# Eight layer norms move from the third block of a Fourier layer into the first stage of its fourth block

## The chip, the cores and the metric

The kernel runs on one core of a Trainium2 chip. The metric is device time in microseconds: the median over executions. Before the change it is 1607.54 us, the median of 3 executions from 1606.18 to 1608.23.

## The reference

The program applies four layers to one sequence of S = 2048 rows and D = 512 columns, in f32: two pairs of a Fourier layer (FNet) and a gated feed-forward layer (GEGLU, F = 1792). Each layer normalises its input rows first and adds its result to the input.

```python
def fnet(x, Sre, Sim, Hre, Him):        # y = Re(DFT_seq(DFT_hid(x)))
    a, b = x @ Hre.T, x @ Him.T
    return Sre @ a - Sim @ b
def geglu(x, wg, wu, wd):
    return (gelu(x @ wg) * (x @ wu)) @ wd
x = x + fnet(layernorm(x), ...)         # layer 0
x = x + geglu(layernorm(x), ...)        # layer 1
x = x + fnet(layernorm(x), ...)         # layer 2
x = x + geglu(layernorm(x), ...)        # layer 3
```

`layernorm` takes mean and variance over the 512 columns of a row and has no weights; eps is 1e-5.

## The kernel before

**Products.** Every f32 operand x is split into two numbers, hi (a copy rounded to a narrower type, by ScalarE, line 168; line 194 is the form with the sign turned) and lo = x - hi (by VectorE, line 170; with the sign turned, line 196). A product is three matmuls into the same bank: hi by hi (line 225), hi by lo (226), lo by hi (227), each of a 128x128 weight by 128x512. So a matmul of line 225 needs ScalarE's half alone, and those of 226 and 227 need VectorE's as well. On top of that the kernel multiplies 2x2 blocks of matrices with seven block products in place of eight, for which sums and differences of blocks (VectorE, line 201 plus of SBUF tiles, line 205 the same plus where one operand is a PSUM bank, line 208 minus) are formed on the way. ScalarE copies finished banks out in line 212.

**Layer 2 in blocks.** The function `mix` runs a Fourier layer. Its output rows come in four blocks b = 0 to 3 of 512 rows; the change is about the third (b = 2) and the fourth (b = 3) of layer 2. A block has two stages:

- S2, 24 steps of six matmuls (function `six`): three chains of eight steps (T2, T1, T3), skewed against each other, each with two banks of its own. The rows of the sequence DFT that it multiplies (`ws` in the trace) come by DMA through SP's queue (line 348), and are summed (line 201 and 208), then split. When the first chain ends, ScalarE copies its banks (line 212) and the banks of the second are added to the copies (line 205).
- S4, 16 steps: two chains (B22, T4) into the banks that S2's second and third chain left.

Between the blocks stand products with the hidden DFT (weights `wq`), for two blocks at a time, named P1 to P7. Block 3 has four of P7 early and, after S4, its last products: two each of P4, P7, P4. The operands of P4 and P7 come from the banks that S4 leaves. The remaining twelve (P6, P5, P3) run beside the next layer.

**The next layer's first half.** Layer 3 takes its rows in two halves of 1024. To begin, it needs the first half normalised and transposed (z^T), and that work is done beside layer 2's last blocks. The function `block_steps` makes the pieces, for row tiles i = 0 to 7 of 128 rows:

- `ahead`, a load of row tiles (line 253, 256 KB each): tiles 4 to 7 through POOL's DMA queue, tiles 0 to 3 (called L in the table of the change) through SP's;
- `stats(i)` (A in the table): VectorE takes the statistics of a tile (line 643) and gathers them (645), adds eps (649); POOL raises the result to the power -1/2 (650); VectorE makes the shift (654);
- `norm(i)` (B): ScalarE scales and shifts the tile (line 687), VectorE transposes it in pieces of 32 (line 780) into one of two tiles named `wide`; after the fourth transpose of a tile, POOL issues the write of it, 1 MB, to DRAM (line 783);
- `fetch(c)`, c = 0 to 3: 8 DMAs on POOL (line 794, 64 KB each, four from each of the two writes) that bring a column block of z^T back.

Behind them VectorE forms differences and sums of the fetched tiles, and both engines split them, for layer 3's first products.

**Where they stand.** Two lists spread this work. `chores` is walked by blocks 2 and 3 at 16 places of a block: two early products, eight steps of S4, six late products. `queue` gives one entry per step of matmuls (function `step`). Before, block 2's chores were: the row loads, nothing, then eleven entries of statistics and norms (`NORM_STEPS`); the queue of block 3's S2 held eight empty entries, and then fetches and empty entries by turns. The wrapper `paced` keeps such an entry behind the newest split on ScalarE and VectorE.

**What sets the order.** These lists give the order in the program text. The order on each engine is then set at compile time by a scheduler that goes by a model of the time line, within the data's dependences and the order constraints (`issue_after`, `behind`, `paced`). Each engine works through its own row in order, so whatever waits at its head holds all behind it.

Two other loads touch the place: `xwide` and `wide`, 1 MB each (line 974, four DMAs on SP), bring the layer's old rows back, to which the products of a pair of blocks are added.

Of the kernel before, what the change touches and what calls it, by code (L numbers as in the profile page):

```python
# [21 lines left out]
NT = TB // P  # L22
# [26 lines left out]
PAIRED = {2: ((0, 1), (2, 3))}  # L49
BESIDE = 2  # L50
FURTHER = 4
NORM_STEPS = (
    (("A", 4),), (("A", 5),), (("B", 4), ("A", 6)), (("B", 5), ("A", 7), ("L", 0)), (("B", 6), ("L", 1)),
    (("B", 7), ("A", 0), ("L", 2)), (("A", 1), ("L", 3)), (("B", 0), ("A", 2)), (("B", 1), ("A", 3)), (("B", 2),), (("B", 3),),
)
FIRST_SUMS = 9, 10
LATER = 3
LET = 5
# [6 lines left out]
def fnet_geglu(ctx: ExitStack, tc: tile.TileContext, x_in, ws, wh, wgu, wdn, wdc, whc, out):  # L65
# [32 lines left out]
    nc = tc.nc  # L98
# [73 lines left out]
    def paced(run):  # L172

        def paced_run():
            with tc.issue_after(newest["ACT"].ins), tc.issue_after(newest["DVE"].ins):
                run()
        return paced_run
# [431 lines left out]
    queue, slow, steps_done, pace, down_making = [], [], [0], [PACE], []  # L609
# [264 lines left out]
    def mix(layer):  # L874
        hid, sums, chores, hid_left = {}, {}, [], [0]

        def chores_at(b):
            if b == NB - 3:
                norms, others = block_steps(layer + 1, 0)
                at = 0 if b in paired else NT  # L880
                if not at:
                    ahead = begin[layer + 1, 0, "ahead"]
                    stats = begin[layer + 1, 0, "stats"]
                    both = {("A", i): paced(stats(i)) for i in range(2 * NT)}
                    both.update({("B", i): paced(norms[i]) for i in range(2 * NT)})
                    both.update({("L", i): lambda i=i: ahead(i, 1, nc.sync) for i in range(NT)})

                    def several(*names):
                        return lambda: [both[name]() for name in names]

                    norms = [lambda: ahead(NT, NT, nc.gpsimd), lambda: None]
                    norms += [several(*names) for names in NORM_STEPS]
                later.update(norms=norms[at:], fetches=others[:ND], others=others[ND:])
                return norms[:at]
            if b == NB - 2:
                weights = [weight_steps(n) for n in range(2)] if layer == 0 else []
                norms = later.pop("norms")
                later["others"] += weights[1][1] if weights else []
                return [run for load, _ in weights for run in (load,)] + norms + (weights[0][1] if weights else [])
            return later.pop("others") if b == NB - 1 else []  # L900
# [31 lines left out]
        paired = {b for p in PAIRED.get(layer, ()) for b in p}  # L932
# [24 lines left out]
        def pair_sums():  # L957
            c = sums_due.pop(0)
            u, v = xu.pop(c), xv.pop(c)
            minus(u, cs["P5", c], u)  # L960
            with behind("DVE"):
                nc.vector.scalar_tensor_tensor(v, v, -1.0, u, op0=ALU.mult, op1=ALU.subtract)
            cs["P6", c], cs["P3", c] = u, v
# [60 lines left out]
        def pair_rest(i):  # L1024
            if sums_due:
                pair_sums()
            if i in FIRST_SUMS:
                first_sum(FIRST_SUMS.index(i))
            pair_product(*PAIR_REST[i])
# [106 lines left out]
        sides, us, later = {}, {}, {}  # L1136

        def s2(b):
# [11 lines left out]
            one, three = [ps8.get() for _ in range(2)], [ps8.get() for _ in range(2)]  # L1150
            sides[b] = one, three
            if last:
                queue.extend([None] * (8 if paired else 14) + [run for fetch in later.pop("fetches") for run in (None, fetch)])
            for j, (i, k) in enumerate(skewed(3)):
                if rest_beside(layer, b) and j % BESIDE == 0:
                    pair_rest(j // BESIDE)
# [717 lines left out]
```

## Time and profile before

| | |
|---|---|
| median of 3 executions | 1607.54 us (1606.18 to 1608.23) |
| the profiled execution: its own time, and the span of its instructions | 1609.84 us, 1608.1 us |
| mean granted clock of TensorE | 0.995 of full speed |
| TensorE (PE) busy | 1591.6 us, 99% of the span, 6960 matmuls |
| VectorE (DVE) busy | 1189.1 us, 74% |
| ScalarE (ACT) busy | 881.6 us, 55% |
| GpSimd (POOL) busy | 316.5 us, 20% |
| moved by DMA | 432.79 MB, 269 GB/s over the span |

The profile is one execution. A row that begins with a time is one instruction or a run of equal ones (x6): its start, how long it was busy, the engine, the line of the kernel, and what it reads and writes (out<-in). Square brackets hold the idle time of the engine just before it and what ended that. A row that begins with a line number is a group: how often, its busy time with the mean of one in ns, and the idle time ahead of it with what ended most of it. Tiles carry the names of the program: `s` is any of the 98 work tiles of 128x512, `p` a PSUM bank, `wide`, `rstd`, `shift`, `st` and `mv` are those of the norms. The page gives the span also in 40 slices of 40.2 us, with the busy share in tenths.

### The profile page before, as it was taken

How to read it: one execution, taken by the hardware profiler on the slowest of the kernel's cores; microseconds unless marked ns; L12 is line 12 of the kernel's file. 1: busy time of each engine (PE TensorE's matmuls, PEld its weight loads, DVE VectorE, ACT ScalarE, POOL GpSimd, SP SyncE). 2: the span in 40 equal slices, each digit the busy share in tenths (PEclk: the TensorE clock that was granted, in tenths of full speed). 3: DMA queues.
4: the chain of work that ended last, by engine and by line, in shares of the span. 5: the costliest groups of instructions: out<-in, count | busy, mean ns of one | idle time of the engine just before them, and what ended most of it. 6: DMA issues, size and time to landing. Idle time of an engine off the chain costs nothing.

```text
span 1608.1 us, 22774 instructions
## 1 busy us (share of the span) xinstructions
PE 1591.6 (99%) x6960; PEld 1309.6 (81%) x6960; DVE 1189.1 (74%) x2082; ACT 881.6 (55%) x1687; POOL 316.5 (20%) x533
## 2 busy tenths in 40 slices
PE   9999999999999999999999999998999999999999
PEld 7888888888888888888888888886788888888887
DVE  7997878878699784676868876898795456843573
ACT  8955555654767644656557543545453565333460
POOL 4122322341456101330040000013301000000000
PEclk9999999999999999999999999998999999999999
DMA  9888989976998899997795858787978958996445
GB/s 359 292 328 315 327 307 362 332 263 197 340 322 318 273 322 309 336 345 244 269 304 186 268 169 203 236 271 240 260 268 286 282 170 247 308 277 198 131 144 157
DMA packets 245018, 432.79 MB, mean 269 GB/s; under 512 B 29024, under 2 KB 72288, under 8 KB 243872
## 3 DMA queue, kind: packets, MB, share of 16 engines
q1 hardware_dynamic: 212208, 328.82, 64.1%
q0 software_dynamic: 30000, 100.43, 17.3%
q10 hardware_dynamic: 2688, 2.10, 0.5%
q8 instruction: 55, 0.90, 0.2%
q14 instruction: 67, 0.55, 0.1%
HBM read 333.97 MB, written 97.26 MB: 268 GB/s over the span
## 4 chain that ended last, share of the span: by engine, by line
PE 94%; DVE 2%; DMA 2%; issue 1%; ACT 1%; POOL 0%; SPq 0%; DVEq 0%; POOLq 0%; ACTq 0%
PE p L226 31%; PE p L227 31%; PE p L225 31%; DVE s L170 1%; DMA s<-wq 1%; PE p L1088 1%; DVE s L201 1%; DMA s<-ws 0%; DMA s<-x 0%; PE p L1780 0%; POOL rstd L664 0%; DVE s L205 0%; DVE s L208 0%; DVE wide L780 0%; DVE st L643 0%
## 5 line engine op out<-in xcount | busy, mean ns | idle before, releaser
L226 PE MATMUL p<-s,s 128*128 128x512 f32 x2304 | 896.2, 390 | 4.2 <-DVE s L170 3.5
L227 PE MATMUL p<-s,s 128*128 128x512 f32 x2304 | 890.2, 390 | 0.0
L225 PE MATMUL p<-s,s 128*128 128x512 f32 x2304 | 854.6, 391 | 6.9 <-ACT s L168 4.0
L168 ACT ACTIVATE s<-s 128x512 fp32r<-128x512 f32 (+1 forms) x852 | 480.8, 608 | 299.3 <-DVE s L201 62.2
L170 DVE TENSOR_TENSOR s<-s,s 128x512 fp32r<-128x512 f32 (+1 forms) x852 | 535.9, 661 | 112.1 <-ACT s L168 95.1
L225 PEld LDWEIGHTS p<-s,s 128*128 128x128 f32 x2304 | 433.4, 188 | 100.3 <-ACT s L168 5.7
L226 PEld LDWEIGHTS p<-s,s 128*128 128x128 f32 x2304 | 433.6, 188 | 96.5 <-DVE s L170 5.2
L227 PEld LDWEIGHTS p<-s,s 128*128 128x128 f32 x2304 | 433.6, 188 | 90.5 <-DMA s<-wb 0.3
L205 DVE TENSOR_TENSOR s<-s,p 128x512 f32<-128x512 f32 x211 | 142.3, 682 | 172.1 <-PE p L227 136.3
L201 DVE TENSOR_TENSOR s<-s,s 128x512 f32<-128x512 f32 (+1 forms) x399 | 234.3, 607 | 4.6 <-DMA s<-ws 2.1
L212 ACT ACTIVATE s<-p 128x512 f32<-128x512 f32 x234 | 135.7, 593 | 121.4 <-PE p L227 115.9
L1351 ACT ACTIVATE s<-s 128x512 f32<-128x512 f32 x84 | 52.6, 628 | 42.6 <-DVE s L205 41.7
L334 POOL DMA_DIRECT2D wb<-s x84 | 46.1, 550 | 87.4 <-ACT s L168 68.2
L1351 ACT ACTIVATE s<-p 128x512 f32<-128x512 f32 x28 | 16.7, 597 | 83.3 <-PE p L227 83.3
L687 ACT ACTIVATE s<-s,shift,rstd 128x512 f32<-128x512 f32 x61 | 48.6, 809 | 18.7 <-DVE shift L654 12.3
L1367 DVE TENSOR_TENSOR s<-s,p 128x512 f32<-128x512 f32 x56 | 38.2, 683 | 21.3 <-PE p L227 21.3
L208 DVE TENSOR_TENSOR s<-s,s 128x512 f32<-128x512 f32 (+1 forms) x61 | 36.3, 601 | 22.1 <-DMA s<-ws 17.5
L977 POOL DMA_DIRECT2D x<-wide x8 | 5.2, 658 | 240.3 <-DVE wide L208 240.3
L170 DVE TENSOR_TENSOR s<-xwide,s 128x512 fp32r<-128x512 f32 (+1 forms) x56 | 37.3, 674 | 17.9 <-ACT s L168 12.8
L168 ACT ACTIVATE s<-xwide 128x512 fp32r<-128x512 f32 (+1 forms) x56 | 34.3, 617 | 29.4 <-DVE xwide L205 10.1
L219 ACT ACTIVATE p<-p 128x512 f32<-128x512 f32 x56 | 32.6, 584 | 26.6 <-PE p L227 26.5
L1367 DVE TENSOR_TENSOR s<-s,s 128x512 f32<-128x512 f32 x56 | 38.5, 688 | 1.2
(96 smaller groups left out, 654.0 us busy)
## 6 DMA issues: line engine op xcount, KB each, us to landing
s<-ws SPq DMA_DIRECT2D x368, 256.0 KB, 5.3
s<-wb SPq DMA_DIRECT2D x294, 256.0 KB, 5.2
s<-wc SPq DMA_DIRECT2D x182, 256.0 KB, 4.5
wb<-s POOLq DMA_DIRECT2D x98, 256.0 KB, 4.8
s<-wq SPq DMA_DIRECT2D x56, 256.0 KB, 4.4
s<-x SPq DMA_DIRECT2D x52, 256.0 KB, 5.4
s<-wh SPq DMA_DIRECT2D x52, 256.0 KB, 5.4
wc<-s POOLq DMA_DIRECT2D x49, 256.0 KB, 5.3
```

Source lines behind the costliest of these rows:

```text
L168: newest["ACT"] = nc.scalar.activation(hi, src, AF.Copy)
L170: newest["DVE"] = nc.vector.tensor_tensor(lo, src, f32(hi), op=ALU.subtract)
L201: nc.vector.tensor_tensor(out, a, b, op=ALU.subtract)
L205: bank_read["DVE"] = nc.vector.tensor_tensor(out, a, b, op=ALU.add)
L212: bank_read["ACT"] = nc.scalar.activation(v, src, AF.Copy)
L225: nc.tensor.matmul(ps, ah, bh, start=start, stop=False, skip_group_check=True)
L226: nc.tensor.matmul(ps, ah, bl, start=False, stop=False, skip_group_check=True)
L227: newest["PE"] = nc.tensor.matmul(ps, al, bh, start=False, stop=stop, skip_group_check=True)
L334: nc.gpsimd.dma_start(a, f32(t))
L687: nc.scalar.activation(z, x, AF.Identity, bias=shift, scale=rstd)
L1351: nc.scalar.activation(t, g, AF.Gelu_apprx_tanh)
L1367: nc.vector.tensor_tensor(t, t, v, op=ALU.mult)
```

## The change

The row loads and the statistics of tiles 4 to 7 move to the end of block 2's list (the first eight of its 16 places become empty, then the loads, three empty places, the four statistics). All eight norms, the other four statistics and the loads of tiles 0 to 3 go into a new list, `NORM_LATE`, of twelve entries, which stands at the head of the queue of block 3's S2. The fetches start behind entry 15 of that queue in place of 8.

```diff
-NORM_STEPS = (
-    (("A", 4),), (("A", 5),), (("B", 4), ("A", 6)), (("B", 5), ("A", 7), ("L", 0)), (("B", 6), ("L", 1)),
-    (("B", 7), ("A", 0), ("L", 2)), (("A", 1), ("L", 3)), (("B", 0), ("A", 2)), (("B", 1), ("A", 3)), (("B", 2),), (("B", 3),),
+NORM_STEPS = ((("A", 4),), (("A", 5),), (("A", 6),), (("A", 7),))
+NORM_LATE = (
+    (("B", 4), ("L", 0)), (("B", 5), ("L", 1)), (("B", 6), ("L", 2)), (("B", 7), ("L", 3)),
+    (("A", 0),), (("A", 1),), (("A", 2),), (("A", 3),), (("B", 0),), (("B", 1),), (("B", 2),), (("B", 3),),
 )
+NORM_FROM = 8
+FETCH_AT = 15
@@ chores_at
-                    norms = [lambda: ahead(NT, NT, nc.gpsimd), lambda: None]
+                    norms = [lambda: None] * NORM_FROM + [lambda: ahead(NT, NT, nc.gpsimd)] + [lambda: None] * 3
                     norms += [several(*names) for names in NORM_STEPS]
+                    later["norms late"] = [several(*names) for names in NORM_LATE]
@@ s2
             if last:
-                queue.extend([None] * (8 if paired else 14) + [run for fetch in later.pop("fetches") for run in (None, fetch)])
+                late = later.pop("norms late", [])
+                queue.extend(late + [None] * (FETCH_AT - len(late) if paired else 14) + [run for fetch in later.pop("fetches") for run in (None, fetch)])
```

In the changed kernel the lines above stand three further on (168 becomes 171, 170 becomes 173, 196 becomes 199, 201 becomes 204, 208 becomes 211, 225 to 227 become 228 to 230, 643 becomes 646, 650 becomes 653, 783 becomes 786, 794 becomes 797).

The scheduler answers with another order on every engine. Three places show it. A row gives line, operation, out<-in with the numbers of the tiles, and the shape.

**First place: VectorE at the head of S2 of block 3.** Before (line 643 is a statistic, 196 a lo split for the last of the block before, 201 and 208 sums of S2's rows):

```order
L208 TENSOR_TENSOR s_12355<-s_12353,s_12355 128x512
L208 TENSOR_TENSOR s_12395<-s_12393,s_12395 128x512
L208 TENSOR_TENSOR s_12451<-s_12449,s_12451 128x512
L643 BN_STATS st<-s_12239 128x6
L196 SCALAR_TENSOR_TENSOR s_12350<-s_11947,s_12349 128x512
L643 BN_STATS st<-s_12262 128x6
L643 BN_STATS st<-s_12305 128x6
L196 SCALAR_TENSOR_TENSOR s_12360<-s_11949,s_12359 128x512
L643 BN_STATS st<-s_12322 128x6
L201 TENSOR_TENSOR s_12353<-s_12357,s_12353 128x512
L201 TENSOR_TENSOR s_12393<-s_12397,s_12393 128x512
L201 TENSOR_TENSOR s_12449<-s_12453,s_12449 128x512
```

Now (211, 204, 199 and 646 are those lines, 173 a lo split):

```order
L199 SCALAR_TENSOR_TENSOR s_12271<-s_11949,s_12270 128x512
L204 TENSOR_TENSOR s_12264<-s_12268,s_12264 128x512
L211 TENSOR_TENSOR s_12361<-s_12359,s_12361 128x512
L173 TENSOR_TENSOR s_12366<-s_12280,s_12365 128x512
L204 TENSOR_TENSOR s_12292<-s_12296,s_12292 128x512
L211 TENSOR_TENSOR s_12436<-s_12434,s_12436 128x512
L204 TENSOR_TENSOR s_12268<-s_12266,s_12268 128x512
L204 TENSOR_TENSOR s_12359<-s_12363,s_12359 128x512
L173 TENSOR_TENSOR s_12316<-s_12268,s_12315 128x512
L646 BN_STATS st<-s_12240 128x6
L646 BN_STATS st<-s_12242 128x6
L646 BN_STATS st<-s_12244 128x6
```

Some rows that only repeat line 204 are left out of the second piece. Before, four statistics stood ahead of the first sums of line 201; now sums and two lo splits stand ahead of the first statistic.

**Second place: POOL's row, from the first powers to the last fetch.** Before (650 the powers, 783 the writes of z^T, 794 the fetches, `t_0_1` and `t_0_0` the two halves written):

```order
L650 TENSOR_TENSOR rstd<-rstd,power 128x1 x4
L783 DMA t_0_1_11184<-wide 128x2048
L650 TENSOR_TENSOR rstd<-rstd,power 128x1 x4
L794 DMA s_12622<-t_0_1_11184 32x4x128 x4
L783 DMA t_0_0_11183<-wide 128x2048
L794 DMA s_12687<-t_0_1_11184 32x4x128 x4
```

Now:

```order
L653 TENSOR_TENSOR rstd<-rstd,power 128x1 x4
L786 DMA t_0_1_11184<-wide 128x2048
L653 TENSOR_TENSOR rstd<-rstd,power 128x1
L797 DMA s_12708<-t_0_1_11184 32x4x128 x4
L797 DMA s_12819<-t_0_1_11184 32x4x128 x4
L653 TENSOR_TENSOR rstd<-rstd,power 128x1 x3
L797 DMA s_12780<-t_0_1_11184 32x4x128 x4
L797 DMA s_12742<-t_0_1_11184 32x4x128 x4
L786 DMA t_0_0_11183<-wide 128x2048
L797 DMA s_12703<-t_0_0_11183 32x4x128 x4
```

Before, the second four powers stood ahead of all fetches. Now one of them does, and the other three stand behind eight fetches, which read what the first write writes.

**Third place: TensorE at the last products of block 3** (`p_13138` and `p_13139` are the banks of P4, `p_12839` and `p_12840` those of P7, `p_13242` is the first bank of layer 3). Before, the piece that ends with the two matmuls on `s_13143`, the lo split of an operand of P4 that is made from the banks of S4's chain B22:

```order
L227 MATMUL p_12839<-s_13074,s_12998 128x512
L226 MATMUL p_12840<-s_13075,s_12998 128x512
L227 MATMUL p_12840<-s_13074,s_12998 128x512
L225 MATMUL p_13242<-s_13160,s_13114 128x512
L226 MATMUL p_13242<-s_13161,s_13114 128x512
L227 MATMUL p_13242<-s_13160,s_13115 128x512
L225 MATMUL p_13242<-s_13178,s_13114 128x512
L226 MATMUL p_13138<-s_13143,s_13010 128x512
L227 MATMUL p_13138<-s_13142,s_13010 128x512
```

Now:

```order
L229 MATMUL p_13139<-s_13033,s_12966 128x512
L230 MATMUL p_13139<-s_13032,s_12966 128x512
L228 MATMUL p_13138<-s_13142,s_13010 128x512
L228 MATMUL p_13139<-s_13142,s_13010 128x512
L228 MATMUL p_13242<-s_12853,s_13110 128x512
L229 MATMUL p_13242<-s_12854,s_13110 128x512
L229 MATMUL p_13138<-s_13143,s_13010 128x512
L230 MATMUL p_13138<-s_13142,s_13010 128x512
```

Before, all of P7's last products and 22 matmuls of layer 3 stood ahead of the first use of `s_13143`; now two of layer 3 do, and P7's stand behind. Counted from the last matmul into the first bank of S4's chain B22, 64 matmuls stood ahead of it before, and 32 now.

## The prediction

> **What bounds the kernel now.** I read the page first, then the list of what TensorE waited for, then the time line of the place where it waited. Of the page, the busy line and two of the 40 slices' rows:
>
> ```profile
> PE 1591.6 (99%) x6960; PEld 1309.6 (81%) x6960; DVE 1189.1 (74%) x2082; ACT 881.6 (55%) x1687; POOL 316.5 (20%) x533
> PE   9999999999999999999999999998999999999999
> PEclk9999999999999999999999999998999999999999
> ```
>
> TensorE is the bound, and one slice in 40 (1085 to 1126 us) falls short, in busy time and in granted clock. The waits of TensorE (total, times, longest) and ten-microsecond stretches (first PE busy and its matmuls, then PEld, DVE, ACT, POOL, the clock, DMA) say by how much:
>
> ```profile
> PE p L225 <- ACT s L168: 4.0, 2, 3.3
> PE p L226 <- DVE s L170: 3.5, 2, 2.8
> 1110.00:1120.00 10.00, 6.52 (x14) 4.14 (x14) 8.81 (x23) 6.36 (x12) 8.55 (x8) 0.50 0.09 19
> 1130.00:1140.00 10.00, 10.00 (x45) 8.26 (x44) 7.99 (x13) 4.81 (x8) 6.38 (x12) 1.00 1.06 270
> ```
>
> Fourteen matmuls instead of 45. The time line of TensorE there, at the head of the fourth block's stage S2 (start, duration, idle before and who ended it):
>
> ```profile
> 1094.80 0.39 PE L227 MATMUL p<-s,s 128*128 128x512 f32 x1
> ...
> 1099.56 0.39 PE L227 MATMUL p<-s,s 128*128 128x512 f32 x1
> 1099.79 1.52 PE L225 MATMUL p<-s,s 128*128 128x512 f32 x6
> ...
> 1106.36 0.39 PE L227 MATMUL p<-s,s 128*128 128x512 f32 x1
> 1110.06 1.22 PE L225 MATMUL p<-s,s 128*128 128x512 f32 x2 [3.31 <-ACT s L168]
> 1114.04 0.79 PE L226 MATMUL p<-s,s 128*128 128x512 f32 x1 [2.75 <-DVE s L170]
> ...
> 1122.36 0.80 PE L226 MATMUL p<-s,s 128*128 128x512 f32 x1 [0.75 <-DVE s L170]
> ...
> 1126.36 0.61 PE L227 MATMUL p<-s,s 128*128 128x512 f32 x1
> 1126.79 0.42 PE L225 MATMUL p<-s,s 128*128 128x512 f32 x1
> ...
> 1164.67 0.70 PE L225 MATMUL p<-s,s 128*128 128x512 f32 x2 [1.83 <-DMA s<-wq]
> ```
>
> From 1094.80 to 1099.56 there are 21 steps: 0.2267 us a matmul. After the gap of 3.31 us they come every 0.43 us, at half the clock, until 1126.4. What the other engines did:
>
> ```profile
> 1098.39 1.88 DVE L170 TENSOR_TENSOR s<-s,s 128x512 fp32r<-128x512 f32 x3
> 1103.19 1.28 DVE L643 BATCH_NORM_STATS2 st<-s 128x6 f32<-128x512 f32 x2
> 1107.38 0.37 DVE L645 BATCH_NORM_AGGREGATE mv<-st 128x2 f32<-128x6 f32 x4
> 1107.67 0.66 DVE L201 TENSOR_TENSOR s<-s,s 128x512 f32<-128x512 f32 x1
> 1113.30 1.89 DVE L170 TENSOR_TENSOR s<-s,s 128x512 fp32r<-128x512 f32 x3
> 1121.62 4.29 DVE L170 TENSOR_TENSOR s<-s,s 128x512 fp32r<-128x512 f32 x7
> 1131.24 0.69 DVE L208 TENSOR_TENSOR s<-s,s 128x512 f32<-128x512 f32 x1 [5.33 <-DMA s<-ws]
> 1172.67 1.28 DVE L205 TENSOR_TENSOR s<-s,p 128x512 f32<-128x512 f32 x2 [2.04 <-PE p L227]
> ```
>
> VectorE had no pause from 1098.39 to the sum (1107.67) that the hi split needs, and the lo split came at 1113.30: four statistics (L643) lay between. Seven operations in 4.29 us, the last 0.66 long: 0.605 us each back to back; a small one takes 0.09. That is the bound here: VectorE's queue.
>
> What this stall cost: the six L225 in a row at 1099.79 are found once in the order. From there to the last product of S4's first half, which the pair at 1172.67 reads, the order has 250 matmuls: 56.7 us at 0.2267. They took 72.8. So **16.1 us** are lost in this stretch, 1.83 of them by the wait for wq.
>
> **The change, part by part.** It removes no arithmetic. All eight norms leave the third block's S4 and last products and enter the 24 steps of the fourth block's S2; the thirty-two fetches of z^T come seven steps later. Per norm VectorE does a statistic and a transpose of 0.6 us back to back and three small operations, in all 1.5 us; groups of lines from 1080 to 1180 us:
>
> ```profile
> L780 DVE STREAM_TRANSPOSE wide<-s 128x512 f32<-128x512 f32 x8 | 5.4, 698 | 0.5 <-ACT s L687 0.5
> L643 DVE BATCH_NORM_STATS2 st<-s 128x6 f32<-128x512 f32 x8 | 5.4, 687 | 1.1 <-DMA s<-x 1.1
> ```
>
> Four norms (6 us) go from before the stall to behind it. In exchange the sums of S2 stand ahead of the statistics (first place of the order), and TensorE has 42 instead of 30 matmuls before the first that needs such a sum, so the gap of 3.31 us goes.
>
> *Term 1, S2 itself.* From the last reading of S4's banks to the lo split that the last pair of S2's first chain needs, VectorE's queue now holds 60 large and 21 small operations: 60 x 0.605 + 21 x 0.09 = 38.2 us. It starts at 1098.4 as before, or 2.3 us earlier, since ten matmuls have moved behind S4's end; I take 1097.2. Idle time adds: five shifts that wait for POOL's power, by
>
> ```profile
> 1115.64 0.16 DVE L654 SCALAR_TENSOR_TENSOR shift<-mv,rstd 128x1 f32<-128x1 f32 x1 [0.46 <-POOL rstd L650]
> L650 POOL TENSOR_TENSOR rstd<-rstd,power x4: 548/556/565, 1086.5 to 1089.2; 128x1 f32<-128x1 f32 x4
> L650 POOL TENSOR_TENSOR rstd<-rstd,power x4: 542/626/4659, 1111.0 to 1116.8; 128x1 f32<-128x1 f32 x4
> ```
>
> 5 x 0.46 = 2.3, and a wait for S2's rows behind the 1 MB load of xwide, between 0 and the 5.33 above; I take 2. So 1097.2 + 38.2 + 4.3 = 1139.7, where TensorE, unhindered, would come at 1099.8 + 152 x 0.2267 = 1134.3: **5.4 lost** (bounds: early start, no idle 0; late start, all idle 9.9). The first power took 4.66 us while VectorE ran without a break, the others 0.55 to 0.63.
>
> *Term 2, the chain's end.* S2's first chain ends, ScalarE copies it (line 212), and VectorE adds the second chain's bank to it (line 205). The next matmul writes into that second bank. Before, 29 others stood between (6.6 us); now it comes at once.
>
> ```profile
> L212 ACT ACTIVATE s<-p 128x512 f32<-128x512 f32 x234 | 135.7, 593 | 121.4 <-PE p L227 115.9
> L168 ACT ACTIVATE s<-s 128x512 fp32r<-128x512 f32 (+1 forms) x852 | 480.8, 608 | 299.3 <-DVE s L201 62.2
> ```
>
> A copy, 0.59, and a sum, 0.64, take 1.4 with the hand-overs; two more operations of VectorE stand ahead of the second lo split, 1.2 less one matmul: **2.4** (1.4 to 3.2).
>
> *Term 3, POOL's queue.* The last three powers are now behind eight fetches (second place of the order):
>
> ```profile
> 1115.84 2.93 ACT L687 ACTIVATE s<-s,shift,rstd 128x512 f32<-128x512 f32 x4 [3.00 <-DVE shift L654]
> 1128.76 3.25 POOL L794 DMA_DIRECT2D s<-t  x6 [0.55 <-issue]
> t<-wide POOLq DMA_DIRECT2D x2, 1024.0 KB, 8.8
> s<-t POOLq DMA_DIRECT2D x32, 64.0 KB, 6.3
> ```
>
> The fourth transpose stands behind 48 large and 12 small operations: 1097.2 + 30.1 + four shifts and part of the wait, 3.1, is 1130.4. The write of z^T lands 0.6 + 8.8 later, eight fetches issue in 8 x 0.55, three powers take 1.9, three norms on ScalarE 3 x 0.73 and a split 0.6: 1149. TensorE comes at 1139.7 + 0.9 + 2.4 + 12 x 0.2267 = 1145.7. Behind the waiting shifts stand all of VectorE's splits. **3.3** (0, if the write lands early, to 6).
>
> *Term 4, the last products.* A product of P4 needs a lo split (L196 before, L199 now) of a sum that starts from those finished S4 banks. VectorE's queue holds 19 large operations from the reading of the first of these banks to that split, 11.6 us with the hand-over; before, 18. But before 64 matmuls (14.5 us) stood between on TensorE, and it did not wait; now 32 (7.25 us, third place of the order): 4.4. Two more lo splits behind it cost 1.7 and 1.4 in the same way (17.0 against 15.3, 19.4 against 18.0 us). **7.5** (6.5 to 9.5: the second write of z^T starts near 1151 and lands at 1160, its first fetch 2.2 + 6.3 later at 1168.5; VectorE wants it at 1168, so it may wait up to 2).
>
> *Term 5, the clock.* A gap of 1.83 changed no clock, one of 3.31 did. Term 4's 4.4 us will; half rate there is mostly hidden, as VectorE still sets the pace: **0.8** (0 to 5).
>
> The other late fetches I cost at nothing: the first use of one on VectorE stands 23 large operations behind the chain's end, 1140.6 + 1.4 + 14.1 = 1156, and the third tile, the one it needs, lands at 1146.2 + 2.2 + 6.3 = 1154.7. Without that cover, 1 us late costs 1 us. On SP's queue six loads of wq now stand ahead of the 1 MB load of wide instead of behind it, so I let the 1.83 go; the x rows stand singly among S2's loads, which term 1's wait covers.
>
> Sum: 5.4 + 2.4 + 3.3 + 7.5 + 0.8 = 19.4 lost in place of 16.1 and 0.2 later: +3.1 us. The profiled execution took 1609.84 (span 1608.1), 2.3 over the median of 1607.54; the sum moves all three alike: 1607.5 + 3 = **1610.5 us**.
>
> **The rivals.** *The clock falls twice* (slower). Where the wait in term 1 is one gap of 3.3 us or more, the 28 matmuls that stand behind it run at 0.43. In the trace half rate lasted until 4.0 us of unbroken work were done (1122.36 to 1126.4): 9 matmuls at 0.2 us more are 1.7, and 0.9 more than term 5 has at the end. With xwide's 5.33 in full, 3.3 + 1.7 + 0.9 = 5.9 more: 1616. For it: the clock's fall at 3.31. Against: term 1's waits may come in small pieces. The Trainium skill (TensorE: Matmul & The Clock Gate, Part 1, What's actually happening) puts the point at an idle window of about 3.4 us, which the trace's 3.31 and 1.83 agree with; an estimate from it, half a window lost behind term 4's gap, makes term 5 1.7 and the forecast 1611.4.
>
> *VectorE keeps ahead* (faster). It starts at 1096, loads are there in time, and the powers slip into gaps: term 1 0.9, term 2 2.4, term 3 0.5, term 4 6.5, together 10.3, 6 us less than 16.3: 1601.5. It decides where terms 1 and 3 together stay below 5.4. For it: no x rows in the load queue before S2. Against: 38.2 us of queue over 34.5 us of matmuls. The Trainium skill (GPSIMD Engine Reference, 1. Specifications) says that POOL shares its SBUF interfaces with VectorE and contends with its two-input operations; the 4659 ns agree, and by that rule the powers find no gap, the 2.3 us stay, and this case is 1603.8.
>
> *The stall only moves* (no change): VectorE's large operations from the same start to the split in term 4 are 115 before and 114 now, so if its idle time stays as it was, the end stays: 1607.5.
>
> **How the numbers follow.** The forecast 0.50, with its own range 1607 to 1614; the clock 0.21; VectorE ahead 0.20; only moved 0.09. A range of 1603 to 1616.5 leaves out about a tenth on each side: half of the faster case, half of the clock's. What a measurement here can tell from no change is 0.2%, 3.2 us. Faster by more: the faster case and a little of the forecast's lower end, 0.21. Within: all of the last and 0.28 of the forecast, whose centre lies at +3: 0.37. Slower: the clock's and 0.21 of the forecast, 0.42.
>
> **What would show it.** No wait of 3.3 us for L168 near 1107 (the gain is real); waits at half of S2 and at the chain's end; a wait for the shifts behind the fetches near 1146; a wait of about 4.4 us for the lo split of P4 (now line 199) after 1170, with the clock below 1 behind it. It is wrong if S2 of the fourth block loses under 6 us, or if that last wait is missing: then the change is faster. If VectorE waits for z^T, the fetches decide, not the norms.

## The result and the profile after

The changed kernel takes **1623.79 us** (median of 4 executions, 1620.34 to 1625.14) against 1607.88 for the kernel before on the same chip (4 executions): a ratio of 1.009, 95% interval 1.0068 to 1.0111. It is slower by 15.9 us. The forecast was 1610.5 with a range of 1603.0 to 1616.5, so the direction was right and the size was not: the time lies 7.3 us above the range.

The profiled execution of the changed kernel took 1625.14 us, its span is 1623.4. Its page, the three lines that answer to those shown of before:

```profile
PE 1593.4 (98%) x6960; PEld 1310.8 (81%) x6960; DVE 1190.0 (73%) x2082; ACT 881.4 (54%) x1687; POOL 312.8 (19%) x533
PE   9999999999999999999999999997969999999999
PEclk9999999999999999999999999999989999999999
```

The work of every engine is the same to 4 us. Two slices fall short in place of one, and the deeper one is later: the slice of 1177 to 1218 us, behind S4, where the kernel before had no gap over 0.2 us. The waits of TensorE (total, times, longest):

```profile
PE p L228 <- DMA s<-wb: 12.1, 1, 12.1
PE p L229 <- DVE s L173: 9.1, 4, 6.5
PE p L228 <- DVE s L208: 1.5, 1, 1.5
```

The old wait for line 168's hi split (3.3) is gone, as the prediction said. In its place stand 9.1 us for lo splits, and a wait of 12.1 us that no part of the prediction names: `wb`, a weight of layer 3. The time line of TensorE at these places (start, duration, idle before it and who ended it):

```profile
1111.17 0.50 PE L229 MATMUL p<-s,s 128*128 128x512 f32 x1 [1.58 <-DVE s L173]
...
1134.33 0.80 PE L229 MATMUL p<-s,s 128*128 128x512 f32 x1 [6.50 <-DVE s L173]
...
1148.66 0.47 PE L228 MATMUL p<-s,s 128*128 128x512 f32 x1 [1.50 <-DVE s L208]
...
1192.46 0.76 PE L228 MATMUL p<-s,s 128*128 128x512 f32 x1 [12.05 <-DMA s<-wb]
```

**Where the time went.** From the starts of all matmuls in the two traces one can add up by how much each stands more than 0.2267 us behind the one before it. From 1095 to 1205 us this gives 17.3 us for the kernel before and 33.1 for the changed one, and the difference is that of the spans (15.3) to half a microsecond. The rows leave out steps of under 0.1 us:

| place | before | after |
|---|---|---|
| S2 of block 3, first half and its lo splits, with half clock | 14.3 | 12.0 |
| S2, the chain's end and the late shifts | 0 | 4.8 |
| wait for wq behind the load of wide | 2.0 | 0 |
| end of S4 and first products of layer 3 | 0.6 | 15.9 |

Up to 1175 us both kernels stand level: the matmul that started at 1175 before starts 0.3 us later after. So all the loss is in the last row: 12.05 us of waiting for one weight, and some 3 us at half clock behind it.

**Why that weight was late.** SP's queue, first of the kernel before, then of the changed one:

```profile
1160.80 0.32 SPq L1341 DMA_DIRECT2D s<-wb  x1
...
1166.73 5.52 SPq L1341 DMA_DIRECT2D s<-wb  x11
```

```profile
1163.91 2.32 SPq L978 DMA_DIRECT2D wide<-x  x4
1167.83 1.56 SPq L351 DMA_DIRECT2D s<-wq  x1
1169.49 0.54 SPq L1346 DMA_DIRECT2D s<-wb  x1
1170.12 1.01 SPq L351 DMA_DIRECT2D s<-wq  x1
1171.18 12.68 SPq L1346 DMA_DIRECT2D s<-wb  x9
1184.20 2.40 SPq L351 DMA_DIRECT2D s<-wq  x4
1186.98 1.00 SPq L1346 DMA_DIRECT2D s<-wb  x2
```

The profile's rows don't tell which tile each load fills; the order on SP does (place in the row, line, tile and source; the first number in a name is the work tile, the second numbers the uses):

```
before  913 L1341 DMA s81_13110<-wb0_185 128x512
        917 L1341 DMA s4_13114<-wb0_185 128x512
after   915 L1346 DMA s16_13114<-wb0_185 128x512
        917 L1346 DMA s46_13122<-wb0_185 128x512
        ...
        930 L1346 DMA s7_13110<-wb0_185 128x512
        931 L1346 DMA s9_13111<-wb0_185 128x512
```

`13110` and `13111` are hi and lo of the first weight pair that layer 3 multiplies with. Before, its hi half led the weights, issued at 1160.8. After, ten other weights stand ahead of it; it goes out with its lo half in the pair issued from 1186.98, and TensorE starts again 5.5 us later.

The tiles tell why the scheduler put it there. The list of free tiles hands out the one that was given back first in the program's text, and in both kernels the first weight pair gets tiles into which fetches bring z^T: 81 and 68 before, 7 and 9 after (`s7_12708` and `s9_12780` on POOL's row). The load has to wait until VectorE has read its tile for the last time, and that reading came later. For the hi half's tile, in the order and in the trace:

```
before  L201 s97_12992<-s68_12687,s81_12622
after   L204 s23_12932<-s7_12708,s50_12703
```

```profile
1159.12 0.68 DVE L201 TENSOR_TENSOR s<-s,s 128x512 f32<-128x512 f32 x1
```

```profile
1174.06 0.69 DVE L204 TENSOR_TENSOR s<-s,s 128x512 f32<-128x512 f32 x1 [0.42 <-DMA s<-t]
```

After, the last reading is a sum with a fetch of the second write of z^T, which the late norms moved from 1121 to 1156, and it stands behind the first sum of S4's banks. Tile 9 is read for the last time until 1177.2. Even so both tiles were free some ten microseconds before the pair was issued: what held the load was its place behind ten others in the queue.

The kernel before had no room here either. Its lo half stood thirteenth of the weights, landed at 1179.7, and TensorE's weight load waited 0.3 us for it:

```profile
1179.78 0.19 PEld L227 LDWEIGHTS p<-s,s 128*128 128x128 f32 x1 [0.31 <-DMA s<-wb]
```

### The profile page after: what moved, and what is told of

It is laid out like the page before. It is cut to its first block, busy times and chain, and to the rows that moved or that the text cites. A ratio compares the mean times of both kernels' runs of the same rounds, so it can differ in the third digit from the quotient of the medians.

```text
span 1623.4 us, 22765 instructions
## 1 busy us (share of the span) xinstructions
PE 1593.4 (98%) x6960; PEld 1310.8 (81%) x6960; DVE 1190.0 (73%) x2082; ACT 881.4 (54%) x1687; POOL 312.8 (19%) x533
## 3 DMA queue, kind: packets, MB, share of 16 engines
q0 software_dynamic: 30000, 100.43, 17.3%
## 4 chain that ended last, share of the span: by engine, by line
PE 92%; DMA 4%; DVE 2%; ACT 1%; issue 1%; POOL 0%; SPq 0%; DVEq 0%; ACTq 0%; POOLq 0%
PE p L229 31%; PE p L230 30%; PE p L228 30%; DMA s<-ws 2%; DMA s<-wb 1%; DVE s L173 1%; DMA s<-wq 1%; DVE s L204 1%; PE p L1092 1%; DMA s<-x 0%; ACT s L171 0%; POOL rstd L667 0%; DVE s L211 0%; DVE wide L783 0%; ACT s L690 0%
## 5 line engine op out<-in xcount | busy, mean ns | idle before, releaser
L228 PE MATMUL p<-s,s 128*128 128x512 f32 x2304 | 854.1, 391 | 15.4 <-DMA s<-wb 12.1
```

Of the source, the lines that this page charges most:

```text
L228: nc.tensor.matmul(ps, ah, bh, start=start, stop=False, skip_group_check=True)
```

## The experiments

Each time is a median, each ratio goes against runs of the kernel before on the same chip. The kernel before had medians of 1607.9 to 1609.4 beside them, so ratios compare better than times. Single executions of several kernels spread by up to 0.6%, and a profile is one of them. "Lost" is the sum over matmul starts, as in the table above.

### Other tiles for the first weights

```diff
                 if layer:
+                    ints = [i for i, n in enumerate(sb.free) if isinstance(n, int)][:14]
+                    turn = [sb.free[i] for i in ints]
+                    for i, n in zip(ints, turn[2:] + turn[:2]):
+                        sb.free[i] = n
                     weight_load(0)
```

> The changed kernel, with the free list of work tiles turned by two places just before the fourteen first weight loads of layer 3, so that the first weight pair no longer takes the two tiles that z^T leaves last. SP's row keeps its form, but its first weight load is now the tile that TensorE uses first (in the changed kernel that tile is the eleventh of them). Theory A (tile reuse and order): the wait of 12.1 us for wb at 1180 goes, since the load at this place was issued at 1169.5 and landed some 7 us later. TensorE then meets the lo split of P4, which VectorE ends at 1184.9 in the changed kernel's trace: a wait of about 4 us near 1181, 6 to 8 us lost with its echoes and the clock. Time 1614 us (1611 to 1617), 10 under the changed kernel. Theory B (the loads as a whole are late, since the 1 MB load of wide and sixteen fetches share the DMA engines with them): another weight is late in its place, TensorE waits 8 to 12 us for wb there, and the time stays at 1620 to 1624.

Measured: 1615.65 us, ratio 1.0045 (1.0032 to 1.0058), 8 us under the changed kernel (its profiled execution, 1620.03, is the slowest of five, and 2 us late ahead of S2 already). TensorE's gaps behind S4:

```profile
1182.04 0.47 PE L228 MATMUL p<-s,s 128*128 128x512 f32 x1 [1.42 <-DVE s L173]
1187.47 0.80 PE L230 MATMUL p<-s,s 128*128 128x512 f32 x1 [4.73 <-DMA s<-wb]
```

The hi half came in time; the wait of 12 us became 4.7 for the lo half, which stood fifth of the weights on SP's row. Theory A has the time, but B is not out: a weight was late in its place. (The load at the head of the weights took 11.2 us to land in the changed kernel, not the 7 that the expectation gives it.) Apart from these loads the edit moved twelve matmuls and two operations of ScalarE in the engines' orders, all beside the first weights. The next run gives both halves tiles that are free early, and changes nothing else (against the run above):

```diff
-                    for i, n in zip(ints, turn[2:] + turn[:2]):
-                        sb.free[i] = n
+                    for i, n in zip(ints, (2, 6, 7, 8, 3, 4, 5, 9, 10, 11, 12, 13, 0, 1)):
+                        sb.free[i] = turn[n]
```

> The changed kernel with another permutation of the fourteen work tiles that the first weights of layer 3 take: both halves of the first weight pair now get tiles that are free early, so that they are the first and the second of the weights on SP's row. In the run that turned the list by two, the hi half came first and TensorE still waited 4.7 us for the lo half, which stood fifth. Theory A (which tile the first pair gets, and so its place on SP's row): no wait for wb is left, TensorE goes on to the lo split of P4 and waits there for VectorE alone, 2 to 4 us with half the clock behind it for one or two steps of 3.4 us: 1612 to 1615 us, 1 to 4 below the run that turned the list. Theory B (the loads as a whole are late behind the 1 MB load of wide): the second half waits all the same, 3 to 5 us, 1615 to 1617 us.

Measured: 1615.55 us, ratio 1.0037 (1.0025 to 1.0049); applied to the 1607.9 beside the changed kernel that is 1613.8, in A's range, while the time as measured lies in B's. The step from the run above is not clear of noise, since the two intervals overlap; that from the changed kernel is. The same place in its trace:

```profile
1178.13 0.47 PE L228 MATMUL p<-s,s 128*128 128x512 f32 x1 [0.61 <-DMA s<-wb]
1180.31 0.50 PE L230 MATMUL p<-s,s 128*128 128x512 f32 x1 [1.49 <-DMA s<-wb]
1182.78 0.50 PE L229 MATMUL p<-s,s 128*128 128x512 f32 x1 [1.27 <-DVE s L199]
```

Of the 12.05 us 2.1 are left, and behind them shows what they had hidden: the wait for the lo split of P4 (line 199), which the prediction's term 4 named. The end of S4 loses 7.8 us here, against 15.9. So some 8 us of the change's loss hang on which tile a weight got. B holds for the 2.1 that are left: the pair was issued at 1168.0 and 1169.6 and took 10.0 and 10.7 us to land, where the median of these loads in this trace is 5.2. The DMA engines' share in the ten-microsecond stretches of 1160 to 1190 is 1.05 to 1.08; that this is the reason is not shown.

### The row loads of tiles 0 to 3

In S2 of the changed kernel SP stood for 9.2 us at one row load, with S2's rows behind it, and VectorE then waited for these. SP's longest wait, and VectorE's rows:

```profile
SPq L256 <- DVE mv L648: 9.2, 1, 9.2
```

```profile
1130.60 0.69 DVE L204 TENSOR_TENSOR s<-s,s 128x512 f32<-128x512 f32 x1 [5.12 <-DMA s<-ws]
...
1147.82 0.69 DVE L208 TENSOR_TENSOR s<-s,p 128x512 f32<-128x512 f32 x1 [5.61 <-ACT s L215]
```

Two runs take these loads away from there, one to POOL's queue, one to the third block's list:

```diff
-both.update({("L", i): lambda i=i: ahead(i, 1, nc.sync) for i in range(NT)})
+both.update({("L", i): lambda i=i: ahead(i, 1, nc.gpsimd) for i in range(NT)})
```

> The changed kernel, with the loads of row tiles 0 to 3 issued by POOL's queue in place of SP's. In the changed kernel SP stood 9.2 us (1106 to 1116) at one of these loads, which waited for a tile that a split of S2 frees, and behind it stood S2's own rows; VectorE waited 5.1 us for these and TensorE 6.5. Theory C (SP's queue made the wait in S2): the wait of 6.5 us for the lo split near 1128 goes, and with it the half clock behind it (5.5 us at half rate, 2.7 us): 6 to 9 us less, 1615 to 1618; the wait for wb stays at 10 to 12, since the first weight pair is still behind others on SP's queue. Rival D (VectorE's own queue bounds S2, as the prediction's term 1 had it): VectorE's wait for rows goes, but TensorE still waits 4 us or more for lo splits in S2, and the gain is under 4 us: 1620 to 1624.

```diff
-NORM_STEPS = ((("A", 4),), (("A", 5),), (("A", 6),), (("A", 7),))
+NORM_STEPS = ((("A", 4), ("L", 0)), (("A", 5), ("L", 1)), (("A", 6), ("L", 2)), (("A", 7), ("L", 3)))
-    (("B", 4), ("L", 0)), (("B", 5), ("L", 1)), (("B", 6), ("L", 2)), (("B", 7), ("L", 3)),
+    (("B", 4), ), (("B", 5),), (("B", 6),), (("B", 7),),
```

> The changed kernel with the row loads of tiles 0 to 3 in the third block's list (on SP's queue, beside the statistics of tiles 4 to 7), and not in S2; all norms stay late. SP then meets these loads before S2's rows that are needed late. If the load that waited 9.2 us for a tile on SP's queue made S2's wait of 6.5 us (theory C), that wait shrinks to 3 us or less, as the run with these loads on POOL's queue did not fully show (it kept 4.9); time 1615 to 1619, since the wait for wb stays. If VectorE's own queue bounds S2 (rival D): waits for lo splits of 4 us or more stay there, and the time is 1620 to 1624.

Measured: 1621.61 us, ratio 1.0081 (1.0069 to 1.0093), and 1618.74 us, ratio 1.0058 (1.0044 to 1.0071). S2, its chain's end included, lost 16.8 us in the changed kernel. It loses 18.4 with the loads on POOL and 13.9 with the loads early, and in both the waits for lo splits stay:

```profile
1132.54 0.80 PE L229 MATMUL p<-s,s 128*128 128x512 f32 x1 [4.85 <-DVE s L173]
...
1189.89 0.77 PE L228 MATMUL p<-s,s 128*128 128x512 f32 x1 [8.46 <-DVE s L173]
```

```profile
1119.23 0.73 PE L228 MATMUL p<-s,s 128*128 128x512 f32 x2 [2.93 <-ACT s L171]
1121.25 0.79 PE L229 MATMUL p<-s,s 128*128 128x512 f32 x1 [1.28 <-DVE s L173]
1144.93 0.80 PE L229 MATMUL p<-s,s 128*128 128x512 f32 x1 [3.58 <-DVE s L173]
```

The first pair of rows is of the run with POOL's queue, the second group of the run with early loads. The first has the time that rival D gave (1620 to 1624) and a wait of over 4 us for a lo split; the second has C's time (1615 to 1619), and its longest wait for one, 3.58, lies between the two forecasts. So C against D stays undecided; at best 3 us of S2's loss came from these loads. On POOL a row load waited 8.8 us for the same operation of VectorE. In that run the chain of waits leads over two fetches of z^T (8.1 and 5.9 us to landing) and VectorE to TensorE's gap of 8.5 us, with the weight no longer the last to come. Both edits together, POOL's queue and the turned list:

> Both edits on the changed kernel: the turned free list and the row loads on POOL's queue. If theories A and C hold and their effects add: neither the wait of 6.5 us in S2 nor the one of 12.1 for wb; what is left is the lo split of P4, 4 us with echoes: 1605 us (1601 to 1610), at or below the kernel before. If B or D holds for either: 1612 us or more.

Measured: 1616.77 us, ratio 1.0051 (1.0039 to 1.0063): no better than the turned list alone (1.0045), and 12 us over the 1605 that the sum of two theories gave. No wait for wb was left in the profiled execution, and VectorE took its place:

```profile
1179.82 0.76 PE L228 MATMUL p<-s,s 128*128 128x512 f32 x1 [3.09 <-DVE s L204]
1188.78 0.50 PE L229 MATMUL p<-s,s 128*128 128x512 f32 x1 [1.03 <-DVE s L173]
```

### One half of the change at a time

First the late fetches alone, on the kernel before:

```diff
-queue.extend([None] * (8 if paired else 14) + ...
+queue.extend([None] * (15 if paired else 14) + ...
```

> The kernel before, with only the fetches of z^T seven steps later (behind 15 entries in place of 8); the norms stay in the third block. In this order the first weight tile of layer 3 is the first of the weights on SP's queue, as before. Theory A: no wait for wb above 1 us, and the time is that of before, 1608 us (1606 to 1611), with the old waits of 3.3 and 2.8 at S2's head. If the late fetches alone make the loss (VectorE waits for z^T, and what follows is late): a wait of VectorE for z^T of 3 us or more, and 1612 to 1620.

Measured: 1611.71 us, ratio 1.0021 (1.0011 to 1.0031); its executions lie from 1608.60 to 1615.25. The profiled one (1609.23) shows S2's old gaps (3.31 and 3.24 us), no wait for wb and a span 0.6 us under that of before. So the fetches alone don't make the loss: the second write of z^T, and with it VectorE's last reading of the first weights' tiles (1159.7 for the hi half's), stayed early. The median lies between the ranges of the two theories; the 0.2% has no place in this profile, and stays unexplained.

Then half of the norms: tiles 4 to 7 as before, only tiles 0 to 3 late, with all row loads in the third block and the fetches behind entry 8 again (against the changed kernel; the old tables are left out):

```diff
+NORM_STEPS = ((("A", 4),), (("A", 5),), (("B", 4), ("A", 6)), (("B", 5), ("A", 7), ("L", 0)),
+    (("B", 6), ("L", 1)), (("B", 7), ("L", 2)), (("L", 3),))
+NORM_LATE = ((("A", 0),), (("A", 1),), (("A", 2),), (("A", 3),), (("B", 0),), (("B", 1),), (("B", 2),), (("B", 3),))
+FETCH_AT = 8
-                    norms = [lambda: None] * NORM_FROM + [lambda: ahead(NT, NT, nc.gpsimd)] + [lambda: None] * 3
+                    norms = [lambda: ahead(NT, NT, nc.gpsimd), lambda: None]
```

> Only half of the norms is late: tiles 4 to 7 stay in the third block with the row loads of all eight, as before; the statistics and norms of tiles 0 to 3 go into the first eight entries of the queue of block 3's S2, and the fetches start behind entry 8, as before. Theory E (before, the four statistics of tiles 0 to 3 at S2's head made the gaps of 3.3 and 2.8 us; in the changed kernel the work for tiles 4 to 7 came late for nothing, since VectorE was idle 6.8 of 10 us in 1080 to 1090 and then behind to the end of S4): S2 loses 4 to 8 us less than in either kernel, the second write of z^T starts some 10 us later than before, not 35, and the time is 1600 us (1596 to 1605). Rival F (VectorE's queue over S2 and S4 holds the same work wherever the norms stand, and a stall moves): 1606 to 1612 us.

Measured: 1610.12 us, ratio 0.9999 (0.9990 to 1.0008). By the time, rival F. By the trace, theory E and a new wait: S2 loses 3.8 us in place of 14.3 and 16.8, and TensorE led the kernel before by 10.6 us until 1150. Then:

```profile
1156.69 1.22 PE L225 MATMUL p<-s,s 128*128 128x512 f32 x2 [6.29 <-ACT s L194]
```

```profile
1141.36 1.96 SPq L975 DMA_DIRECT2D wide<-x  x4
1143.42 2.81 SPq L348 DMA_DIRECT2D s<-ws  x1
1146.34 0.59 SPq L348 DMA_DIRECT2D s<-wq  x1
1147.02 0.38 SPq L348 DMA_DIRECT2D s<-ws  x1
```

The 1 MB load of wide now stood ahead of the last rows of S4; the chain of waits has the last of them landing 8.95 us after 1147.02, a hi split of ScalarE behind it, and TensorE behind that. The same half with the fetches at entry 12:

> The same half, with the fetches of z^T behind entry 12 of the queue in place of 8. In this order the first weight tile of layer 3 is the fifth of the weights on SP's row, not the first. Theory E: as in the run with entry 8, 1600 us, up to 3 more if the weight is late. Theory A says that later fetches hold the tiles longer in which the first weights land: a wait for wb of 2 to 6 us near 1170, and 1603 to 1608. Rival F: 1608 to 1614.

Measured: 1611.88 us, ratio 1.0015 (1.0006 to 1.0024). S2 loses 10.3 us here, with a gap of 6.6 for a lo split (VectorE waited 4.8 for a row of S2), and a weight half was late by 2.0 at 1178. The time, 1611.9, is that of F (1608 to 1614); the weight's wait is that of A. Why S2's rows were late in this order was not followed further. It matters: the same four norms late, with later fetches, leave S2 only 4 us better than before.

### What the late half is worth when the loads stand right

The load of wide at step 10 of S4 in place of 5, and at 8:

```diff
-WIDE_AT = 14, 5
+WIDE_AT = 14, 10
```

> The kernel with half of the norms late (tiles 0 to 3), and the 1 MB load of wide asked for at step 10 of block 3's S4 in place of step 5. In the run with half the norms late, TensorE was 10.6 us ahead of the kernel before until 1150, and then waited 6.3 us for a hi split whose row of the DFT matrix stood behind the load of wide on SP's queue (8.95 us to its landing). Theory G (the gain in S2 is real and was given back at this load): with the load behind all rows of S4 that wait goes, the lead of 7 to 10 us lasts, and the time is 1601 us (1598 to 1604), 0.3 to 0.6% under the kernel before. Rival H (a lead in S2 is lost at the end of S4 whatever the load does, since VectorE's queue or the weights on the DMA engines, at 390 GB/s before, set that end): other waits take its place, 1606 to 1610.

> The same with the load of wide at step 8 (on SP's queue it stands behind four loads of hidden-DFT weights and ahead of the first weights of layer 3, in place of behind nine loads). Theory G: as with step 10, 1601 us (1598 to 1604). Rival H: 1606 to 1610.

> The kernel before, with only the load of wide at step 10 of S4. It tells what this move is worth alone. In the kernel before, the load stood behind all rows of S4 already, and TensorE waited 1.8 us for hidden-DFT weights behind it. Theory G: that wait goes and S2's waits stay: 1606 us (1604 to 1609), so that what the runs with half the norms late gain above this comes from S2. If the move itself is what gains: 1603 or less.

Measured: 1605.77 us, ratio 0.9985 (0.9974 to 0.9995) with step 10; 1606.44 us, 0.9988 (0.9979 to 0.9996) with step 8; and the kernel before with step 10 alone 1610.27 us, 1.0010 (1.0001 to 1.0019). Faster, but by a third of what theory G gave: the times are those of rival H, or just under them. The move alone, on the kernel before, gains nothing, where 1606 was expected: the wait for wq went, and one of 1.39 us for wb came. The profiled execution of step 10 is the fastest of its nine (1603.31). In it the lead over the kernel before holds until 1165 and reaches 13.0 us, of which 1.9 stood already ahead of S2; 6.6 are then given back at one place:

```profile
1171.26 0.80 PE L227 MATMUL p<-s,s 128*128 128x512 f32 x1 [3.06 <-DMA s<-wb]
```

It is the same fault as in the changed kernel, at a smaller price: the lo half of layer 3's first weight pair had been given a tile that comes free late, and stood twelfth of the weights on SP's row (the expectation below counts tenth). In the kernel before it stood thirteenth, and TensorE reached it just as it landed, so a lead gained ahead of it runs into a wait for it. So the last run exchanges tiles once more; the engines keep their orders, and on SP's row the weights change places among themselves (`ints` and `turn` as in the first run):

```diff
+                    for i, n in zip(ints, (0, 2, 3, 4, 5, 6, 7, 8, 9, 10, 11, 12, 13, 1)):
+                        sb.free[i] = turn[n]
                     weight_load(0)
```

> The kernel with half of the norms late and the load of wide at step 10, with one more edit: of the fourteen tiles for layer 3's first weights, the lo half of the first pair takes the third in place of the second, so that on SP's row it stands second of the weights in place of tenth. The orders of all engines stay as they were. In the run without it TensorE led the kernel before by 13.0 us until 1165, and lost 6.6 at a wait of 3.1 us for that lo half and in the 6.8 us of half clock behind it. Theory A: the wait goes, TensorE keeps 3 to 6 us of the 6.6, up to a wait for the next lo split, and the time is 1601 us (1598 to 1603.5), 0.3 to 0.6% under the kernel before. Theory B (the weights are late as a whole, since they share the DMA engines with the load of wide): another weight is late and the time stays at 1605 to 1607.

Measured: **1600.25 us** (1599.99 to 1600.80), ratio 0.9945 (0.9931 to 0.9960): 8.7 us under the 1608.98 beside it, the fastest kernel of this case. Two rows of its page, and the first four of TensorE's waits:

```profile
PE   9999999999999999999999999999999999999998
PEclk9999999999999999999999999999999999999999
```

```profile
PE p L225 <- DMA s<-wq: 2.1, 2, 1.3
PE p L1786 <- POOL ident masks.py:199: 1.4, 1, 1.4
PE p L225 <- ACT s L168: 1.2, 1, 1.2
PE p L226 <- DVE s L170: 0.9, 1, 0.9
```

No slice before the last falls short, and no wait is over 1.4 us. Theory A predicted this time before the run, for an edit that decides only which tile a weight lands in.

## Why the prediction was wrong

Point by point, its sums against the table:

- **Term 1**, S2 bound by VectorE's queue: 5.4, measured 12.0 with the half clock behind it. The mechanism is there (waits for lo splits in S2's middle), the size was off by 6.6. VectorE's wait for rows of S2 was taken as 2 of a bound of 5.33; it was 5.12, in one piece. So TensorE's gap was one of 6.5 us, which the rival "the clock falls twice" had described with 3.3: the ten-microsecond stretch behind it ran at a granted clock of 0.51.

```profile
1130.00:1140.00 10.00, 5.67 (x14) 4.49 (x15) 9.13 (x23) 1.15 (x2) 2.25 (x4) 0.51 0.64 233
1180.00:1190.00 10.00, 0.41 (x2) 0.00 (x0) 10.00 (x18) 3.12 (x6) 0.00 (x0) 0.71 1.05 352
```

- **Terms 2 and 3**, the chain's end and POOL's queue: 2.4 + 3.3 = 5.7, measured 4.8. That these are close is partly luck. The chain's end is there: VectorE's row at 1147.82 stood 5.6 us waiting for ScalarE's copy, and TensorE's waits of 1.50 and 0.64 behind it come to 2.1. Of term 3 at most a wait of 0.27 shows: the late powers began at 1143.57, behind eight fetches as said, but the shifts that need them did not hold TensorE. Much of the rest is 3.41 us at half clock, some 1.7 by an estimate from that record, which neither term had.
- **Terms 4 and 5**, P4's lo split and the clock: 7.5 + 0.8. In the changed kernel the end of S4 lost 15.9, and no wait for line 199 shows, since VectorE, busy for all of 1180 to 1190 (second row above), worked it off while TensorE waited for the weight. (So the prediction's own sign, that the change is faster if this wait is missing, failed too.) With the weight in time (the run with both halves first) the end loses 7.8, close to the 8.3 predicted, but again partly by luck: the wait for line 199 was 1.27 in place of 4.4, two waits for wb of 2.1 together stood ahead of it, and 3.41 us ran at half clock.
- **The step that failed** is the sentence "The other late fetches I cost at nothing". It checked whether VectorE would get z^T in time, and VectorE did: it waited 0.4 us. It did not ask when VectorE reads the tiles of z^T for the last time, and who gets them next. That is where the loss came in: the sums with the second write of z^T now stand behind the first of S4's banks, layer 3's first weight pair was loaded into two of their tiles, and the load stood behind ten others. The late fetches alone left the weight in time, so it takes the late norms and their second write; the late norms alone were not run. Beside it, the paragraph on SP's queue counted wq and wide, and not the weights of layer 3 behind them. In numbers: with other tiles the changed kernel comes to 1613.8 us, inside the range.
- **The whole difference**: 19.4 us of loss were predicted for the changed kernel, and the table has 32.7. Of the 13.3 between them 7.6 stand at the end of S4 (15.9 for 8.3), 6.6 in term 1, and 0.9 less in terms 2 and 3.
- **The direction** was right, and by luck in part. S2 was to gain 5 us, with the wait for wq counted to it, and lost half a microsecond; the loss at the end of S4 that terms 4 and 5 gave shows only where the weight is in time.
- **"The stall only moves"** describes S2 better than the forecast did: up to 1175 us the two kernels differ by 0.3 us. It was given a chance of 0.09, with a queue of 114 against 115 operations as its reason; that this is why S2 came out level is not shown.
- **"VectorE keeps ahead"** fell, but half of the change does what it described: with four norms late, not eight, S2 loses 3.8 us. The likely reason is the norms of tiles 4 to 7: VectorE (third pair of columns) was idle for most of 1080 to 1090 in the changed kernel, where before it was busy for 7.31 us of 10, and the same work then stood in S2. It is not shown alone, since that run also has the row loads early and the fetches at entry 8, and with the fetches at entry 12 S2 loses 10.3.

```profile
1080.00:1090.00 10.00, 10.00 (x46) 8.29 (x45) 3.22 (x6) 1.20 (x2) 3.72 (x6) 1.00 0.96 289
```

What stays open: how much of S2's 12.0 us is VectorE's own queue and how much late rows. The two runs that moved the row loads disagree (18.4 and 13.9 with the chain's end, against 16.8), since each moved other waits too.

## What to carry to other kernels

When a transfer is moved later, ask of its tile what is asked of its data: who is given that memory next, and what stands behind that load in its queue. Where a list of free tiles hands out what was given back first in the program's text, the most urgent load can get the tile that comes free last; giving it another one adds no work and was worth some 8 us here, and 5.5 us on the way to the fastest kernel (6.4 by the ratios). And a move that fills a tight stage is worth trying by halves: four norms moved gained 10 us in S2 with the fetches where they were, eight with later fetches gained nothing.

## What was not expected of the hardware

- The granted clock fell behind shorter gaps than the 3.31 us on which the prediction built. In the changed kernel two waits of 1.50 and 0.64 us, both between 1147.1 and 1149.8, were followed by a stretch at half clock:

```profile
1150.00:1160.00 10.00, 9.73 (x35) 7.41 (x35) 9.24 (x19) 5.49 (x10) 2.73 (x5) 0.83 0.62 194
```

In the run with the fetches at entry 12 waits of 1.97 and 0.67 us did the same, while the 1.83 us of the kernel before did not, nor did 1.50 and 0.64 in the run with the turned list. In the traces' record of the granted clock, from 60 us on, all such stretches, but for the one that the program's end cuts off, are 3.41, 6.83, 10.24, 13.65 or 17.07 us long: whole multiples of 3.41. Their starts lie on the same grid: 1129.58, 1150.06 and 1184.19 in the changed kernel are six and ten steps of 3.41 apart. The Trainium skill (TensorE: Matmul & The Clock Gate, Part 1, What's actually happening) has a free-running window of 3.4 us; the traces agree with it, and by that rule where a gap falls counts as well as how long it is.
- How much idle time it takes can be counted, by cutting the thirteen traces that have such a stretch into intervals of that grid, again from 60 us on. Every interval at full clock with 1.92 us or more of TensorE's idle time was followed by half clock, and none with 1.58 or less; between 1.69 and 1.84 both happened. So it was about half of an interval, not a whole one. The two waits of the changed kernel put 2.14 us into one interval; the 1.83 us of the kernel before lay across two, with 1.55 in the fuller one. Half clock went on after an interval with 0.67 us of idle time or more, and ended after one with 0.21 or less.
- A load on SP's queue took 4.4 to 5.4 us to land over most of the program (the medians on the page of the kernel before). In the changed kernel it took 7.2 (median of wb from 1155 to 1195), beside a 1 MB load and the fetches: the four weights issued first behind that load took 11.2 to 12.3 us, the last four 5.3.
